# First MLP: the rest of the second half of each weight tile, taken by an accumulating DMA

## The chip, the cores and the metric

The kernel runs on one core of one Trainium2 chip. The metric is the device time of one execution in microseconds (us); a comparison goes by the median of several executions. The trace is one profiled execution, and every time in it counts from the start of its span.

The engines go by the profile's names: PE (TensorE's matmuls), PEld (its weight loads), DVE (VectorE), ACT (ScalarE), POOL (GpSimd), SP (SyncE). Each works through its own list of instructions in order; semaphores tie the lists together.

## The reference

Attention over 4 sequences of 576 rows with 8 heads (a window of 128, a bias that falls with distance), then a first MLP, then a layer of 8 experts that routes each of the 2304 rows to one expert of capacity 288. The change touches the first MLP alone:

```python
def _moe_ref(x, w_in, w_out, alpha):
    h = x @ w_in                                   # 2304 x 512 @ 512 x 2048
    g = np.maximum(h, 0.0) + alpha * np.minimum(h, 0.0)
    return (g @ w_out).astype(np.float32)          # 2304 x 2048 @ 2048 x 512
```

## The kernel before

**Tiles.** The first MLP's hidden dimension is cut into 16 tiles `f` of 128. Tile `f` of the weights is one array of 128 partitions by 1024 numbers: its first half (columns 0 to 511) is the part of `w_in`, its second half (512 to 1023) the part of `w_out`. The rows of `x` are cut into 9 units `u` of 256.

**Splitting.** The weights lie in memory as 64-bit numbers, and the matmuls take pairs of float32r parts: `wh` (a weight, rounded) and `wl` (the rest, weight minus `wh`). `load_w64` fetches 1 MB, one tile, as 16-bit words (`raw`); one transfer of SP's queue for tiles 0 to 2, of ACT's queue for the others. `split_w64_(f, i)` then makes half `i` of tile `f`: DVE takes the top words of both halves at once (L144, or L142 for each half of tile 15), ACT makes the first bits of `w` (L149), DVE adds the mantissa (L150) and the sign (L151), ACT writes `wh` as a rounded copy of `w` (L152), and POOL writes `wl` as `w - wh` (L153). `w` is tile `w64w`, of which there are two buffers, under the tag that the output tiles `y` use later. Tile 15 is loaded in two halves of 0.5 MB through one buffer (`raw15_0`, `raw15_1`); the constants `ramps` (an IOTA of POOL, L722) take that buffer afterwards.

**Work.** `l1(u, f)` is 12 matmuls of 256 columns (`wh` with `xh`, `wh` with `xl`, `wl` with `xh`) on the first half; ACT (L557) and DVE (L558) make the activation `g` from it, ACT the rounded `gh` (L561), and for units 0 and 1 POOL the rest `gl` (L565). `l2(u, f)` multiplies `gh` and `gl` with the second half of the tile, `wh` and `wl`. Units 0 and 1 alternate over the tiles, unit 0 four tiles ahead: `l1(0, f)` is number `2f - 2` of these steps from tile 4 on. So tile 9 comes into use at the 16th `g`, tile 11 at the 20th, tile 15 at the 28th. From the 33rd on, units 2 to 8 use weights that are all there.

**Order.** The attention of later blocks goes on among these steps. The code gives a rough order; a scheduler with its own idea of durations then places each instruction on its engine and assigns the buffers. Of tile `f` from 4 on, the load stands behind the instruction kept in `SPLIT[f - 2]`:

```python
g = LOADED.get(LG_) if f == LF else SPLIT.get(f - LD) if f > LF else None   # LF = 3, LD = 2
with tc.issue_after(g.ins) if g is not None else nullcontext():
    load_w64_(f)
```

## Time and profile before

| | |
|---|---|
| runs | 933.4, 936.16, 939.03 us; median 936.16 us |
| the profiled execution | 942.45 us, of which the span of the trace is 939.7 us |
| PE busy in the span | 846.7 us (90%) |
| DVE, ACT, POOL busy | 626.6 us (67%), 472.7 us (50%), 363.5 us (39%) |
| granted TensorE clock, mean | 0.942 |

The shares are averages over an attention stage with the first MLP (to about 580 us) and an expert stage behind it. The change works in the first 165 us, so what counts is which engine is full there, and for what PE waits there.

### The profile page before, as it was taken

What the parts mean: (1) busy time and instruction counts of PE and PEld (TensorE: products, weight loads), DVE (VectorE), ACT (ScalarE), POOL (GpSimd) and SP (SyncE); (2) the same over time, 40 slices, a digit from 0 to 9 for tenths busy, and PEclk for the clock granted to TensorE, in tenths of its full rate; (3) what the DMA queues carried; (4) which work ended last, traced back from release to release, by engine and by line L of the source; (5) the groups of instructions that cost most, each with busy time, mean ns of one, the idle gap of its engine ahead of it and who ended that gap; (6) DMA issues with size and microseconds to landing.
All of it is one profiled execution on the core that took longest, in us unless ns stands there. A gap on an engine that the chain in (4) does not pass through costs nothing.

```text
span 939.7 us, 18007 instructions
## 1 busy us (share of the span) xinstructions
PE 846.7 (90%) x6709; PEld 774.9 (82%) x6709; DVE 626.6 (67%) x1709; ACT 472.7 (50%) x1131; POOL 363.5 (39%) x316
## 2 busy tenths in 40 slices
PE   6797788999999999999999999398979889799996
PEld 4676666888898999899999998387969788699996
DVE  7899996367776877887776544677677666762210
ACT  4787776565655656565655333134325243244541
POOL 5656666421101101110000000196566774659841
PEclk8999999999999999999999999568889889799999
DMA  7753452012211212112010000245343353436510
GB/s 210 250 180 131 144 169 85 20 49 80 73 42 58 74 29 80 58 35 79 13 35 1 19 5 14 80 135 164 129 141 125 107 167 130 120 121 182 180 49 25
DMA packets 33911, 89.00 MB, mean 95 GB/s; under 512 B 7456, under 2 KB 7456, under 8 KB 33824
## 3 DMA queue, kind: packets, MB, share of 16 engines
q1 hardware_dynamic: 28736, 64.79, 22.3%
q10 hardware_dynamic: 2016, 13.63, 4.2%
q0 software_dynamic: 3072, 9.44, 3.2%
q8 instruction: 52, 0.85, 0.4%
q14 instruction: 35, 0.29, 0.1%
HBM read 78.40 MB, written 9.44 MB: 93 GB/s over the span
## 4 chain that ended last, share of the span: by engine, by line
PE 71%; DVE 20%; DMA 3%; SPq 2%; issue 2%; ACT 1%; POOL 0%; POOLq 0%; DVEq 0%; ACTq 0%
PE ph L551 18%; PE py L593 16%; PE pyx L1098 11%; PE phx L1080 10%; DVE cmp L864 5%; PE prt L878 3%; DVE w64w L151 3%; DVE w64w L150 3%; PE S L408 2%; PE py L579 2%; PE pav L502 2%; DVE w64q L144 2%; PE pt L443 1%; PE prt L1002 1%; PE pox L1116 1%
## 5 line engine op out<-in xcount | busy, mean ns | idle before, releaser
L551 PE MATMUL ph<-xh,ws 128*128 128x256 f32 x1152 | 188.0, 286 | 12.1 <-DVE g L558 11.9
L1032 POOL TENSOR_TENSOR ws<-wr,ws 128x512 fp32r<-128x512 f32 x128 | 166.3, 1332 | 55.0 <-ACT ws L1029 54.6
L551 PEld LDWEIGHTS ph<-xh,ws 128*128 128x128 f32 x1152 | 160.0, 190 | 25.8 <-DVE g L558 19.6
L593 PE MATMUL py<-ws,gh 128*128 128x512 f32 x512 | 151.2, 404 | 1.5 <-ACT gh L561 1.5
L343 POOL TENSOR_TENSOR ks<-kr,ks 64x512 fp32r<-64x512 f32 x34 | 51.5, 1518 | 217.5 <-ACT ks L342 197.9
L558 DVE SCALAR_TENSOR_TENSOR g<-ph,sa_sb,g 128x256 f32<-128x256 f32 x144 | 68.9, 480 | 75.3 <-ACT g L557 75.0
L557 ACT ACTIVATE g<-ph,sg_sb 128x256 f32<-128x256 f32 x144 | 67.5, 470 | 97.8 <-PE ph L551 94.3
L1098 PE MATMUL pyx<-hh,ws 128*128 128x288 f32 x512 | 116.5, 313 | 0.0
L1029 ACT ACTIVATE ws<-wr 128x512 fp32r<-128x512 f32 x128 | 72.9, 628 | 56.0 <-DMA wr<-in_we_dram 54.3
L593 PEld LDWEIGHTS py<-ws,gh 128*128 128x128 f32 x512 | 88.7, 190 | 14.6 <-ACT gh L561 2.0
L561 ACT ACTIVATE gh<-g,sg_sb 128x256 fp32r<-128x256 f32 x144 | 72.7, 506 | 50.8 <-DVE g L558 27.8
L551 PE MATMUL ph<-xl,ws 128*128 128x256 f32 x576 | 96.4, 282 | 0.0
L1080 PE MATMUL phx<-exh,ws 128*128 128x288 f32 x512 | 92.2, 321 | 0.0
L593 PE MATMUL py<-ws,gl 128*128 128x512 f32 x256 | 89.5, 409 | 1.4 <-POOL gl L565 1.1
L1098 PEld LDWEIGHTS pyx<-hh,ws 128*128 128x128 f32 x512 | 89.9, 200 | 0.0
L551 PEld LDWEIGHTS ph<-xl,ws 128*128 128x128 f32 x576 | 81.7, 190 | 2.2
L864 DVE TENSOR_TENSOR cmp<-ramps,u 128x1280 f16<-128x1280 f16 (+5 forms) x58 | 81.1, 1438 | 0.2
L1080 PEld LDWEIGHTS phx<-exh,ws 128*128 128x128 f32 x512 | 80.2, 207 | 0.4 <-ACT exh L1051 0.3
L1098 PE MATMUL pyx<-hl,ws 128*128 128x288 f32 x256 | 78.7, 307 | 0.0
L567 DVE SCALAR_TENSOR_TENSOR gl<-g,sg_sb,gh 128x256 fp32r<-128x256 f32 x112 | 58.3, 523 | 18.2 <-ACT gh L561 16.1
L878 PE MATMUL prt<-ob,cmp 128*128 128x8 f16 x522 | 38.1, 205 | 35.3 <-DVE cmp L864 32.9
L878 PEld LDWEIGHTS <-cmp 128*128 128x128 f16 x522 | 35.4, 161 | 39.3 <-DVE cmp L864 35.2
(251 smaller groups left out, 1662.2 us busy)
## 6 DMA issues: line engine op xcount, KB each, us to landing
wr<-in_we_dram SPq DMA_DIRECT2D x64, 512.0 KB, 3.6
raw<-in_wm_dram ACTq DMA_DIRECT2D x12, 1023.8 KB, 5.6
kr<-in_k_dram SPq DMA_DIRECT2D x68, 128.0 KB, 2.8
qr<-in_q_dram SPq DMA_DIRECT2D x64, 128.0 KB, 2.7
y_dram<-y SPq DMA_DIRECT2D x18, 256.0 KB, 2.3
vr<-in_v_dram SPq DMA_DIRECT2D x13, 256.0 KB, 3.0
raw<-in_wm_dram SPq DMA_DIRECT2D x3, 1023.8 KB, 8.1
whole<-in_v_dram SPq DMA_DIRECT2D x4, 256.0 KB, 5.6
```

The source lines that it names most:

```text
L551: nc.tensor.matmul(ph, w[f][:, c * P:(c + 1) * P], x[u][:, c, :], start=i == 0, stop=i == 11)
L557: nc.scalar.activation(g, ph, AF.Copy, scale=sg)
L558: nc.vector.scalar_tensor_tensor(g, ph, sa_sb[:, f:f + 1], g, op0=ALU.mult, op1=ALU.max)
L561: nc.scalar.activation(gh, g, AF.Copy, scale=sg)
L567: nc.vector.scalar_tensor_tensor(gl, g, sg, f32(gh), op0=ALU.mult, op1=ALU.subtract)
L593: nc.tensor.matmul(PY[u][i], a[:, s], w[f][:, 512:], start=f == 0 and j == 0, stop=f == FT - 1 and j == 2)
L864: nc.vector.tensor_tensor(cmp[:, :K, cs], th[:, :, :n], u16[:, None, cs].to_broadcast([P, K, n]), ALU.is_le)
L878: nc.tensor.matmul(cnt, cmp[:, :, c], r["ob"][:, c], start=c == 0, stop=c == NB - 1)
L1029: nc.scalar.activation(wh[s][:, h], w[:, h], AF.Copy)
L1032: (nc.vector if on_dve else nc.gpsimd).tensor_sub(wl[s][:, h], w[:, h], f32(wh[s][:, h]))
L1080: nc.tensor.matmul(ph, w[s][:, c * P:(c + 1) * P], x[:, c], start=i == 0, stop=i == 11)
L1098: nc.tensor.matmul(py, w[s][:, cs], r[x][f], start=i == 0, stop=i == 23)
```

## The change

The first half of each tile is made as before. For the second half ACT writes, behind `wh`, a second copy `-w`, rounded in the same way, to the place of `wl`; POOL then issues a DMA that adds `w` to it in SBUF, so that `w - wh` stands there when it has landed. `SPLIT[f]`, behind which the load of tile `f + 2` stands, is now that second copy.

```diff
@@ -150,7 +150,12 @@
         SPLIT[f] = nc.scalar.activation(wh[f][:, s], w, AF.Copy)
-        nc.gpsimd.tensor_sub(wl[f][:, s], w, f32(wh[f][:, s]))
+        if i == 0:
+            nc.gpsimd.tensor_sub(wl[f][:, s], w, f32(wh[f][:, s]))
+        else:
+
+            SPLIT[f] = nc.scalar.activation(wl[f][:, s], w, AF.Copy, scale=-1.0)
+            nc.gpsimd.dma_start(f32(wl[f][:, s]), w, accum_op=ALU.add)
```

The lines below 153 move down by 5 in the changed kernel: L558 becomes L563, L722 becomes L727, and the new copy and the new DMA are L157 and L158.

The first place is DVE about the 16th `g`. Before, it is `g_1247` below, and the halves of tiles 12 to 14 (`raw12`, `raw13`, `raw14`) stand around it:

```order
L150 SCALAR_TENSOR_TENSOR w64w_1381<-raw12_1227,w64w_1381 128x512
L151 SCALAR_TENSOR_TENSOR w64w_1381<-raw12_1227,w64w_1381 128x512
L144 TENSOR_SCALAR w64q_1416<-raw13_1344 128x1024
L558 SCALAR_TENSOR_TENSOR g_1247<-ph_644,sa_sb_100,g_1247 128x256
L150 SCALAR_TENSOR_TENSOR w64w_1418<-raw13_1344,w64w_1418 128x512
L151 SCALAR_TENSOR_TENSOR w64w_1418<-raw13_1344,w64w_1418 128x512
L150 SCALAR_TENSOR_TENSOR w64w_1496<-raw13_1344,w64w_1496 128x512
L558 SCALAR_TENSOR_TENSOR g_1316<-ph_644,sa_sb_100,g_1316 128x256
L151 SCALAR_TENSOR_TENSOR w64w_1496<-raw13_1344,w64w_1496 128x512
L144 TENSOR_SCALAR w64q_1535<-raw14_1424 128x1024
```

In the changed kernel the 16th `g` is `g_1258` on DVE, and the halves around it are those of tiles 9 and 10:

```order
L150 SCALAR_TENSOR_TENSOR w64w_1111<-raw9_982,w64w_1111 128x512
L144 TENSOR_SCALAR w64q_1151<-raw10_1052 128x1024
L151 SCALAR_TENSOR_TENSOR w64w_1111<-raw9_982,w64w_1111 128x512
L150 SCALAR_TENSOR_TENSOR w64w_1153<-raw10_1052,w64w_1153 128x512
L151 SCALAR_TENSOR_TENSOR w64w_1153<-raw10_1052,w64w_1153 128x512
L563 SCALAR_TENSOR_TENSOR g_1258<-ph_648,sa_sb_100,g_1258 128x256
L563 SCALAR_TENSOR_TENSOR g_1328<-ph_648,sa_sb_100,g_1328 128x256
L150 SCALAR_TENSOR_TENSOR w64w_1196<-raw10_1052,w64w_1196 128x512
L144 TENSOR_SCALAR w64q_1230<-raw11_1159 128x1024
L151 SCALAR_TENSOR_TENSOR w64w_1196<-raw10_1052,w64w_1196 128x512
```

The splitting has moved back against the rest. Counted over DVE's whole list, 26 halves (L150) stand ahead of the 16th `g` before and 21 now, 31 and 24 ahead of the 20th, 32 and 28 ahead of the 24th, 32 and 32 ahead of the 28th. What else stands ahead of each of these is the same on PE, DVE and ACT, but for a few rows.

The second place is ACT between two loads. Before, with the semaphores that a row waits for (`Pool` is POOL's, `DVE` DVE's, `DMAHW` a load's), the second half of tile 10 begins (L149 of `w64w_1186`) ahead of the `wh` of its first half:

```order
L149 ACTIVATE w64w_1186<-w64q_1141,least_75 128x512 [waits Pool_49]
L152 ACTIVATE ws10_1140<-w64w_1143 128x512 [waits DMAHW6_49,DVE_49]
L561 ACTIVATE gh_1029<-g_1026,sg_sb_99 128x256 [waits DVE_49]
L564 ACTIVATE g_1026<-g_1026,sg_sb_99 128x256 [waits Activation_49]
L557 ACTIVATE g_1063<-ph_644,sg_sb_99 128x256 [waits PE_49]
L149 ACTIVATE w64w_1221<-w64q_1219,least_75 128x512 [waits DVE_49,Pool_49]
L152 ACTIVATE ws10_1140<-w64w_1186 128x512 [waits DVE_49]
L122 DMA raw12_1227<-in_wm_dram 128x4095 [waits DMAHW2_49]
```

In the changed kernel, on ACT again (`DMASW` is an accumulating DMA's semaphore):

```order
L152 ACTIVATE ws10_1150<-w64w_1153 128x512 [waits DMAHW7_49,DVE_49]
L566 ACTIVATE gh_1261<-g_1258,sg_sb_99 128x256 [waits DVE_49,Pool_49]
L569 ACTIVATE g_1258<-g_1258,sg_sb_99 128x256 [waits Activation_49]
L562 ACTIVATE g_1328<-ph_648,sg_sb_99 128x256 [waits PE_49]
L149 ACTIVATE w64w_1196<-w64q_1151,least_75 128x512 [waits Pool_49]
L566 ACTIVATE gh_1331<-g_1328,sg_sb_99 128x256 [waits DVE_49]
L569 ACTIVATE g_1328<-g_1328,sg_sb_99 128x256 [waits Activation_49]
L149 ACTIVATE w64w_1232<-w64q_1230,least_75 128x512 [waits DMASW1_49,DVE_49]
L562 ACTIVATE g_1376<-ph_648,sg_sb_99 128x256 [waits PE_49]
L152 ACTIVATE ws10_1150<-w64w_1196 128x512 [waits DVE_49]
L157 ACTIVATE ws10_1150<-w64w_1196 128x512
L122 DMA raw12_1238<-in_wm_dram 128x4095 [waits DMAHW3_49]
```

Both halves of a tile now take the same `w64w` buffer, one behind the other: the second half's L149 (`w64w_1196`) stands behind the first half's L152 and waits for POOL's L154 on it; tile 11's first L149 (`w64w_1232`) waits for the accumulating DMA of tile 9; and the load of tile 12 stands behind both copies of tile 10's second half.

The third place is the end of the splitting on POOL. In the changed kernel (before, L153 of `ws15` stands where L158 does now):

```order
L154 TENSOR_TENSOR ws15_1631<-w64w_1634,ws15_1631 128x512
L570 TENSOR_TENSOR gl_1776<-g_1772,gh_1775 128x256
L570 TENSOR_TENSOR gl_1822<-g_1818,gh_1821 128x256
L727 IOTA ramps_3007 128x1280
L727 IOTA ramps_3007 128x768
L570 TENSOR_TENSOR gl_1848<-g_1844,gh_1847 128x256
L158 DMA ws15_1631<-w64w_1713 128x512
```

The last accumulating DMA stands behind the two IOTA and a `gl`, and PE's first product with that part stands behind the 31st `l1` of its list.

## Rows read from the trace of the kernel before

**Rows 1.** The page, section 1: busy us of each engine, share, instructions.

```profile
PE 846.7 (90%) x6709; PEld 774.9 (82%) x6709; DVE 626.6 (67%) x1709; ACT 472.7 (50%) x1131; POOL 363.5 (39%) x316
```

**Rows 2.** By stretch: length; busy PE, PEld, DVE, ACT, POOL; clock, DMA, GB/s.

```profile
60.00:140.00 80.00, 65.86 (x402) 54.21 (x402) 78.69 (x146) 57.14 (x135) 51.96 (x43) 0.96 0.45 149
140.00:165.00 25.00, 21.07 (x123) 16.15 (x123) 17.00 (x25) 16.88 (x34) 15.73 (x13) 1.00 0.27 85
165.00:182.00 17.00, 16.54 (x100) 13.56 (x99) 3.32 (x7) 8.66 (x18) 9.27 (x9) 1.00 0.00 1
```

**Rows 3.** PE's waits from 60 to 140 us: total, times, longest.

```profile
PE ph L551 <- DVE g L558: 5.9, 7, 1.4
PE pav L494 <- DVE et L472: 2.6, 4, 1.5
PE S L408 <- DVE mn L431: 2.1, 3, 1.0
```

**Rows 4.** Groups on DVE from 60 to 140 us: busy, mean ns, idle before.

```profile
L151 DVE SCALAR_TENSOR_TENSOR w64w<-raw,w64w 128x512 uint16<-128x512 uint16 x18 | 20.4, 1134 | 0.1
L150 DVE SCALAR_TENSOR_TENSOR w64w<-raw,w64w 128x512 int32<-128x512 int32 x18 | 17.0, 943 | 0.3 <-ACT w64w L149 0.2
L144 DVE TENSOR_SCALAR w64q<-raw 128x1024 uint16<-128x1024 uint16 x9 | 12.0, 1330 | 0.0
```

**Rows 5.** The splitting's instructions: shortest, median, longest in ns.

```profile
L149 ACT ACTIVATE w64w<-w64q,least x32: 704/712/727, 13.1 to 160.2; 128x512 int32<-128x512 uint16 x32
L150 DVE SCALAR_TENSOR_TENSOR w64w<-raw,w64w x32: 649/830/1753, 13.9 to 161.0; 128x512 int32<-128x512 int32 x32
L151 DVE SCALAR_TENSOR_TENSOR w64w<-raw,w64w x32: 690/1148/1856, 17.3 to 162.3; 128x512 uint16<-128x512 uint16 x32
L152 ACT ACTIVATE ws<-w64w x32: 615/630/640, 19.4 to 163.0; 128x512 fp32r<-128x512 f32 x32
...
L144 DVE TENSOR_SCALAR w64q<-raw x15: 667/694/2224, 12.3 to 145.5; 128x1024 uint16<-128x1024 uint16 x15
```

**Rows 6.** Groups on POOL up to 180 us.

```profile
L153 POOL TENSOR_TENSOR ws<-w64w,ws 128x512 fp32r<-128x512 f32 x32 | 44.5, 1393 | 26.9 <-ACT ws L152 21.5 <-issue 4.9 <-POOL ks L343 0.2
L565 POOL TENSOR_TENSOR gl<-g,gh 128x256 fp32r<-128x256 f32 x26 | 25.9, 1000 | 17.4 <-ACT g L564 11.6 <-issue 3.1 <-POOL ws L153 2.1
...
L722 POOL IOTA ramps<- 128x1280 f16 (+1 forms) x2 | 5.6, 2831 | 0.8 <-DVE w64w L151 0.8
```

**Rows 7.** Timeline, ACT and its queue: the load of tile 13.

```profile
133.06 0.63 ACT L152 ACTIVATE ws<-w64w 128x512 fp32r<-128x512 f32 x1 [0.82 <-DVE w64w L151]
133.07 0.34 ACTq L122 DMA_DIRECT2D raw<-in_wm_dram  x1
```

**Rows 8.** The source line of the loads: shortest, median, longest landing.

```profile
DMA to landing us min/median/max: 4.9/5.9/8.1
```

**Rows 9.** Timeline, DVE: tile 13's first step; the 16th, 28th, 31st g.

```profile
139.02 1.23 DVE L144 TENSOR_SCALAR w64q<-raw 128x1024 uint16<-128x1024 uint16 x1
140.17 0.47 DVE L558 SCALAR_TENSOR_TENSOR g<-ph,sa_sb,g 128x256 f32<-128x256 f32 x1
...
181.10 0.48 DVE L558 SCALAR_TENSOR_TENSOR g<-ph,sa_sb,g 128x256 f32<-128x256 f32 x1 [2.35 <-ACT g L557]
...
191.33 0.48 DVE L558 SCALAR_TENSOR_TENSOR g<-ph,sa_sb,g 128x256 f32<-128x256 f32 x1 [1.98 <-ACT g L557]
```

**Rows 10.** Timeline, expert stage: an issue of POOL, and PE's wait for it.

```profile
611.73 0.92 POOL L1014 DMA_INDIRECT xg<-y_dram,ix  x1 [0.30 <-issue]
...
614.86 0.42 PE L1065 MATMUL ptx<-ident,xg 96*128 96x96 f32 x1 [0.39 <-DMA xg<-y_dram,ix]
```

**Rows 11.** Timeline, ACT's queue and DVE: the second half of tile 15.

```profile
156.02 0.33 ACTq L122 DMA_DIRECT2D raw<-in_wm_dram  x1
...
159.70 0.43 DVE L142 TENSOR_SCALAR w64q<-raw 128x512 uint16<-128x512 uint16 x1 [0.52 <-DMA raw<-in_wm_dram]
...
162.25 0.73 DVE L151 SCALAR_TENSOR_TENSOR w64w<-raw,w64w 128x512 uint16<-128x512 uint16 x1
```

## The prediction

> **What bounds the kernel now.** The page's first section makes PE the full engine over the span [rows 1], so a change matters by the idle time of PE that it takes away or adds. The busy time by stretch says where that is: from 60 to 140 us PE is busy 65.9 of 80 us and DVE 78.7, so DVE is full and PE stands still for 14.1; from 140 to 165 us 3.9 us are left; from 165 us on PE is at 16.5 of 17 and DVE at 3.3, so PE is the bound from there [rows 2]. PE's waits in the first of these stretches name the cause: 5.9 us for DVE's `g`, 2.6 and 2.1 us for other products of DVE, 10.6 together [rows 3]. What fills DVE there is the splitting of the weights: 20.4 + 17.0 + 12.0 = 49.4 of its 78.7 us, for 18 halves [rows 4]. The splitting ends long before it is needed: the second half of tile 15 is done on DVE at 163 us [rows 11], and the 28th `g`, the first that needs tile 15, comes at 181.1 us [rows 9]. So DVE spends the time in which PE starves on weights that are not due yet.
>
> **The sum is made by two clocks:** when the 16th `g` comes (140.2 us before) and when the 28th does (181.1 us) [rows 9]; behind it PE is full in both kernels and the work is the same, so what the 28th gains or loses, the end does.
>
> **Up to the 16th `g`.** A half costs DVE 0.94 + 1.13 + 1.33/2 = 2.74 us [rows 4]. Five fewer stand ahead of it now: 13.7 us. Besides, DVE's instructions of the splitting run at 943, 1134 and 1330 ns here where their shortest take 649, 690 and 667 [rows 4, 5]: 18 x 0.29 + 18 x 0.44 + 9 x 0.66 = 19.2 us above them, while POOL is busy for 52 us [rows 2]. I take POOL's work for the cause, since L151 takes from 690 to 1856 ns at one size [rows 5]. Removing half of the 18 L153 takes 9 x 1.39 = 12.5 us from POOL [rows 6], 24% of its 52, and so 4.6 us from DVE. DVE could give back 18.3 us, more than the 14.1 that PE has idle; but PE waits for DVE in 10.6 us of it alone, and for `g` in 5.9. I take the middle of these two, 8.3 us: the 16th `g` at 131.9 us. Bounds: 5.9 and 14.1. ACT's second copy, 16 x 0.63 us [rows 5], lies in its idle time here (57.1 of 80 us busy [rows 2]); without that cover it were 5 us in this stretch.
>
> **From the 16th to the 28th.** The lead is used up here: 11 halves are left where 6 were, and the changed order makes a loop of each tile. In ACT's list the load of tile `f + 2` stands behind L149 of tile `f + 1`, then L152 and L157 of tile `f`. L149 needs L144 of tile `f + 1`, which needs its load. So from one L144 to the next: L144 0.69, L149 0.71, L152 0.63 [rows 5], then the load, which is issued as the copy ahead of it starts (133.07 beside 133.06 us [rows 7]), and 5.9 us to its landing, the median [rows 8]: 7.9 us. Before, the load of tile 13 stood behind one copy and its L144 followed 5.95 us later [rows 7, 9]. The accumulating DMA sets out right behind the load; it reads 0.25 MB twice and writes it once beside the load's 1 MB. Landings go from 4.9 to 8.1 us [rows 8], so the period is 6.9 to 10.1; I take 8.2, with 0.3 us for the new traffic, since these landings already include other transfers (DMA share 0.45 [rows 2]). The Trainium skill ("DMA: Bandwidth & Descriptors", section "Issuing engines are not separate DMA queues") says that DMAs of all issuing engines run on the same 16 DMA engines and interleave. By that rule the load would be stretched by the other's share of the bytes, up to 0.75 to 1, and a period at its upper bound would cost 4 x 1.9 = 7.6 us more (an estimate); no run here shows it yet. DVE has room in this period: two halves at their shortest and two `g` of 0.47 [rows 9] are 4.3 us.
>
> Tile 11's L144 stands behind the 17th `g`, some 3 us behind the 16th. Four periods later, less 2.2 us because tile 15 comes in halves that take 3.7 instead of 5.9 us [rows 11, 8], is tile 15's first step: 131.9 + 3 + 4 x 8.2 - 2.2 = 165.5. Then 0.43 for it [rows 11], 0.71 + 0.65 + 0.69 + 0.63 [rows 5], 1.39 for POOL's subtraction [rows 6], and 2.35 for the matmuls and ACT's pass, which DVE waits for at the 28th `g` [rows 9]: 6.9 us. The 28th `g` comes at 172.4 instead of 181.1: **8.7 us gained**. The clock was 0.96 and 1.00 in these stretches [rows 2]; I leave it so.
>
> **The end of the splitting.** The last accumulating DMA has two IOTA of 2.83 and a `gl` of 1.0 us ahead of it on POOL [rows 6]. From tile 15's first step: 2.5 us for its first half, 3.7 for the load of the second, 3.3 to the end of its L151 (159.70 to 162.98 [rows 11]), 5.7 + 1.0 on POOL, and the DMA. For that the nearest row is POOL's indirect DMA: from its issue at 611.73, which took 0.92, to PE's start at 614.86 us are 3.1 us [rows 10]. Together 19.3 us. PE wants the part behind the 31st step: 6.9 us to the 28th `g` and 10.2 from there (181.10 to 191.33 [rows 9]), 17.1 us. PE waits 2.2 us; 2.5 with the handing over. What is queued behind it on PE is everything else, so it counts in full.
>
> **The sum:** -8.7 + 2.5 = -6.2 us. Against the profiled execution 942.45 - 6.2 = 936.3; that execution lies above the median of the runs, 936.16, so what I forecast is 936.16 - 6.2 = **930.0 us**.
>
> **The unknown price: the accumulating DMA.** Its time `L`, from issue to landing, is 3.1 us by the row above; from the other side, behind a load that lands late, 0.9 + 8.1 = 9.0. It also holds the buffer: tile `f + 2` begins when that of tile `f` has landed, and until its own lands come L149, L150, L151, L152, the subtraction, L149, L150, L144, L151, L152, L157 and a `gl`, 9.1 us from the same rows, 9.5 with the handing over. So two periods are at least 9.5 + `L` + what each step waits in its engine's line. With 3.1 it is 6.3 us a tile and hidden behind the load's 8.2; it takes over from `L` + waiting = 6.9.
>
> **Rivals.**
> *Slower: the buffer's loop becomes the bound.* Six links wait for another engine, and POOL's subtraction, on which the second half now waits, stands behind `gl`. For it speaks that ACT's L149, when it waits, holds up `gh`, `g` and L152 behind it; against it that DVE is no longer full. With `L` = 9 and 5 us of waiting a tile takes 11.75 us, 3.55 more than in the sum: 14.2 us over four tiles. In the 72 us from 60 us to the 16th `g`, 13 halves (18 less five), 6.5 tiles, would need 76: 4.5 us more. -6.2 + 18.7 = +12.5: 948.7 us. It decides (0.5% slower) from `L` + waiting = 12.3.
> *No change: the same loop at half that.* `L` + waiting = 9.9, a tile in 9.7 us: 4 x 1.5 = 6 us, 936 us. One form of it: POOL's issue is held up beside DVE. L144 has POOL's work beside it when it takes 1.33 instead of 0.67 us [rows 4, 5]; if the issue stands as long, subtraction and `gl` behind it come 1.3 us later each tile, 5 us over four: 935. The Trainium skill ("SBUF — State Buffer", section "SBUF: two separate sides") says that a DVE instruction in a two-port mode keeps GpSimd from writing a DMA's descriptors; no run here shows whether L144 does.
> *More: all idle time of PE comes back.* The 16th `g` at 126.1 us and 7.5 us a tile: the 28th at 163.8, 17.3 us gained, less 2.5: 921.4 us. Against it: a quarter of PE's waits are not for DVE.
>
> **Chances.** The forecast (925 to 935) 0.40, no change 0.25, slower 0.25, more 0.10. About 0.5%, 4.7 us, is what a measurement of this kernel can tell from no change. Of the forecast's 0.40 I put 0.30 below 931.5 and 0.10 above; so faster 0.40, same 0.35, slower 0.25. The range leaves out a tenth at each end: 921 to 947. It takes in the bounds of the 16th `g` and a period of 7.5 to 11.5 us; the forecast's own is 925 to 935.
>
> **What would show it.** Right: the 16th `g` near 132 us, L144 of tiles 11 to 15 some 8 us apart, each about 6 us behind its load; L150 and L151 shorter in the mean; the 28th `g` at 172; one wait of PE of 2 to 3 us for the last accumulating DMA. Wrong: L149 idle for `DMASW` or for L154 in each tile, landings of the accumulating DMA above 7 us, PE's products waiting for them in several tiles; or the 16th `g` where it was, in which case DVE wasn't what PE lacked.

## The result and the profile after

The changed kernel took 942.32 us in the median of 11 runs (939.71 to 949.06), the kernel before 936.31 us in 11 runs on the same chip: a ratio of 1.0068, with a 95% interval of 1.0044 to 1.0093. It is **slower by 6 us**, where 6 us faster was forecast. The profiled execution took 943.4 us, its span 941.7.

The page's first section, to be held against [rows 1]: PE, DVE and POOL are busy for less time, PEld for 2.5 us more, and ACT for 6.1 more with its 16 new copies.

```profile
PE 843.7 (90%) x6709; PEld 777.4 (83%) x6709; DVE 621.1 (66%) x1709; ACT 478.8 (51%) x1147; POOL 349.4 (37%) x316
```

The stretches of [rows 2] in the changed kernel, and one more behind them:

```profile
60.00:140.00 80.00, 68.69 (x450) 59.02 (x448) 68.45 (x146) 62.82 (x147) 44.59 (x45) 0.98 0.59 170
140.00:165.00 25.00, 19.82 (x108) 16.21 (x108) 12.82 (x21) 16.76 (x32) 9.78 (x13) 0.93 0.50 138
165.00:182.00 17.00, 11.92 (x59) 9.72 (x59) 7.36 (x14) 9.57 (x20) 6.14 (x7) 0.90 0.34 72
182.00:260.00 78.00, 74.12 (x622) 65.56 (x621) 56.30 (x161) 47.29 (x121) 19.78 (x15) 1.00 0.22 65
```

The last of these in the kernel before:

```profile
182.00:260.00 78.00, 76.96 (x652) 68.98 (x650) 57.03 (x162) 48.42 (x122) 15.58 (x12) 1.00 0.23 72
```

Two halves show. Up to 140 us the change does what was forecast: DVE falls from 78.7 to 68.5 us and PE rises from 65.9 to 68.7. Behind it PE stands still more than before, 10.3 us instead of 4.4 from 140 to 182 us and 3.9 instead of 1.0 from there to 260, with a DVE that has plenty of idle time. So from 140 to 182 us no engine is full: a chain of waits bounds the kernel there.

PE's waits from 140 to 182 us name the chain (before there was only one kind, for `g`):

```profile
PE ph L556 <- DVE g L563: 5.5, 6, 2.0
PE py L598 <- DMA ws<-w64w: 5.0, 4, 2.6
```

The source line of the accumulating DMA, over the whole span: the issue on POOL, who waited for the landing (us, times), and the time from issue to landing:

```profile
L158 POOL DMA_DIRECT2D ws<-w64w x16: 862/867/1120, 22.8 to 188.4; - x16
...
  PE py L598: 8.3, 7
  ACT w64w L149: 5.6, 5
DMA to landing us min/median/max: 3.7/5.5/7.4
```

A landing takes 3.7 to 7.4 us, inside the bounds of 3.1 to 9.0 that the prediction gave `L`. Both waits that the prediction wrote down as signs against itself are here: ACT's first step of a half waits for it, and PE in several tiles.

**Where the time goes, by stage.** The starts of certain `g` on DVE cut the first stage into pieces that repeat well from one execution to the next. The kernel before was profiled once more (e9 below), the changed kernel twice more: once as it is (e17), once with an edit that alters no order (e1). The later traces come from other chips, on which the kernel before took 941.5 to 942.4 us in the median, not 936.3. All in us:

| | 4th `g` at | 4th to 16th | 16th to 28th | 28th to 144th | from there to the end |
|---|---|---|---|---|---|
| before, two traces | 70.6, 74.5 | 69.6, 70.0 | 40.9, 40.9 | 398.6, 398.3 | 360.0, 360.4 |
| changed, three traces | 65.3, 68.6, 63.3 | 65.1, 64.0, 65.4 | 50.5, 49.5, 49.3 | 403.1, 405.2, 405.1 | 357.6, 362.5, 361.0 |

By the means, 6.8 us are gained to the 4th `g` and 4.9 from there to the 16th; 8.9 are lost from the 16th to the 28th and 6.0 behind it. Together 3.2 us lost, of the 6 that the medians tell; the rest lies within the scatter of the first column, some 4 us for one and the same kernel, and the interval of the medians, 2.3 us to either side.

### The profile page after: what moved, and what is told of

Its sections match the earlier page's. It is cut to its first block, busy times and chain, and to the rows that moved or that the text cites. A ratio compares the mean times of both kernels' runs of the same rounds, so it can differ in the third digit from the quotient of the medians.

```text
span 941.7 us, 18071 instructions
## 1 busy us (share of the span) xinstructions
PE 843.7 (90%) x6709; PEld 777.4 (83%) x6709; DVE 621.1 (66%) x1709; ACT 478.8 (51%) x1147; POOL 349.4 (37%) x316
## 4 chain that ended last, share of the span: by engine, by line
PE 68%; DVE 16%; DMA 7%; ACT 3%; SPq 2%; issue 2%; POOL 1%; POOLq 0%; ACTq 0%; DVEq 0%
PE ph L556 17%; PE py L598 16%; PE pyx L1103 11%; PE phx L1085 8%; DVE cmp L869 6%; DMA ws<-w64w 4%; PE prt L883 3%; PE S L413 2%; PE py L584 2%; DMA vr<-in_v_dram 2%; PE pav L507 2%; DVE w64w L150 1%; PE pt L448 1%; DVE ql L334 1%; DVE g L995 1%
## 5 line engine op out<-in xcount | busy, mean ns | idle before, releaser
L1037 POOL TENSOR_TENSOR ws<-wr,ws 128x512 fp32r<-128x512 f32 x128 | 169.0, 1353 | 46.9 <-ACT ws L1034 46.4
L598 PE MATMUL py<-ws,gh 128*128 128x512 f32 x512 | 156.6, 410 | 9.2 <-DMA ws<-w64w 8.3
L563 DVE SCALAR_TENSOR_TENSOR g<-ph,sa_sb,g 128x256 f32<-128x256 f32 x144 | 69.1, 480 | 73.3 <-ACT g L562 73.0
L598 PEld LDWEIGHTS py<-ws,gh 128*128 128x128 f32 x512 | 89.3, 191 | 25.4 <-DMA ws<-w64w 10.9
L598 PE MATMUL py<-ws,gl 128*128 128x512 f32 x256 | 90.2, 408 | 1.3 <-POOL gl L570 1.0
L1085 PE MATMUL phx<-exh,ws 128*128 128x288 f32 x512 | 88.1, 310 | 0.0
L1085 PEld LDWEIGHTS phx<-exh,ws 128*128 128x128 f32 x512 | 76.3, 198 | 0.4 <-ACT exh L1056 0.3
```

The source lines that it names most:

```text
L563: nc.vector.scalar_tensor_tensor(g, ph, sa_sb[:, f:f + 1], g, op0=ALU.mult, op1=ALU.max)
L598: nc.tensor.matmul(PY[u][i], a[:, s], w[f][:, 512:], start=f == 0 and j == 0, stop=f == FT - 1 and j == 2)
L1037: (nc.vector if on_dve else nc.gpsimd).tensor_sub(wl[s][:, h], w[:, h], f32(wh[s][:, h]))
L1085: nc.tensor.matmul(ph, w[s][:, c * P:(c + 1) * P], x[:, c], start=i == 0, stop=i == 11)
```

## The experiments

The ratios are to runs of the kernel before on the same chip, with 95% intervals; the runs used several chips. Two theories stood from the start. **B** (buffers): the accumulating DMA costs time because it holds a `w64w` buffer, of which there are two, and the next half can't begin. **L** (landing): it costs time because something waits for the landing as such, or for its traffic, wherever the splitting stands. G, A, P, Z and T are named where they were tried.

The table gives what was measured. "Halves" are those ahead of the 16th, 20th and 24th `g` on DVE, and `g` the start of the 28th and of the 144th in the trace.

| run | halves | 28th `g` | 28th to 144th | 144th `g` | ratio |
|---|---|---|---|---|---|
| before (two traces) | 26, 31, 32 | 181.1, 185.4 | 398.6, 398.3 | 579.7, 583.8 | 1 |
| changed | 21, 24, 28 | 180.9 | 403.1 | 584.0 | 1.0068 (1.0044 to 1.0093) |
| e1 gate | 21, 24, 28 | 182.2 | 405.2 | 587.3 | 1.0068 (1.0043 to 1.0093) |
| e2 third buffer | 26, 30, 32 | 178.1 | 398.8 | 576.9 | 1.0014 (0.9993 to 1.0036) |
| e3 no DMA | 31, 32, 32 | 183.6 | 398.6 | 582.2 | 1.0060 (1.0038 to 1.0083) |
| e4 both halves | 21, 25, 29 | 190.5 | 398.1 | 588.6 | 1.0115 (1.0076 to 1.0154) |
| e5 DMA to tile 7 | 22, 27, 31 | 179.4 | 399.6 | 579.0 | 1.0031 (1.0005 to 1.0057) |
| e6 DMA to tile 9 | 21, 25, 30 | 176.9 | 400.4 | 577.3 | 1.0012 (0.9983 to 1.0041) |
| e7 DMA from tile 10 | 26, 29, 32 | 179.7 | 399.4 | 579.1 | 0.9999 (0.9971 to 1.0026) |
| e8 one buffer | 20, 24, 28 | 206.6 | 399.9 | 606.6 | 1.0311 (1.0282 to 1.0339) |
| e10 third buffer late | 22, 27, 31 | 177.7 | 399.6 | 577.3 | 1.0024 (0.9996 to 1.0051) |
| e11 the same, GpSimd late | 22, 27, 31 | 180.3 | 399.9 | 580.2 | 1.0017 (0.9992 to 1.0042) |
| e12 loads earlier | 21, 24, 29 | 177.7 | 402.9 | 580.5 | 1.0071 (1.0046 to 1.0096) |
| e13 DMA to tile 11 | 21, 24, 28 | 179.0 | 399.6 | 578.7 | 0.9953 (0.9922 to 0.9985) |
| e14 tile 15 by GpSimd | 21, 24, 28 | 180.7 | 400.0 | 580.7 | 1.0024 (0.9998 to 1.0050) |
| e15 DMA to 9, loads earlier | 21, 25, 29 | 179.1 | 400.2 | 579.3 | 0.9984 (0.9956 to 1.0011) |
| e16 DMA to 11, gate | 21, 24, 28 | 176.5 | 399.6 | 576.1 | 1.0000 (0.9982 to 1.0018) |
| e17 changed, again | 21, 24, 28 | 178.1 | 405.1 | 583.3 | 1.0061 (1.0030 to 1.0091) |

**e1: the loads' wait undone.**

```diff
-            SPLIT[f] = nc.scalar.activation(wl[f][:, s], w, AF.Copy, scale=-1.0)
+            nc.scalar.activation(wl[f][:, s], w, AF.Copy, scale=-1.0)
```

> The changed kernel, but the load of tile f + 2 stands behind the copy wh again, not behind the second copy -w. Every engine keeps its order; only this wait changes. Theory G (the later load stretches the tiles): each load sets out 0.6 to 1 us earlier, tile 15's first step comes 3 to 5 us earlier, the 28th g near 177 us instead of 181, and the time falls to 937 to 939 us. Theory B (the two w64w buffers, each held by both halves of a tile until the accumulating DMA has landed) and theory L (PE waits for the landing itself) both expect 941 to 943 us, no change against the changed kernel, with ACT's first half still waiting for the accumulating DMA.

1.0068, the changed kernel's ratio again, and the 28th `g` at 182.2 us, not near 177: theory G falls. That the load stands behind one copy more costs nothing that shows.

**e2: a third buffer.**

```diff
-        w = mlp.tile([P, 512], F32, name="w64w", tag="y", bufs=2)
+        w = mlp.tile([P, 512], F32, name="w64w", tag="y" if i else "y2", bufs=2 if i else 1)
```

> The changed kernel with a third buffer for w: second halves take the two that there were, first halves take one of their own, under the tag of a tile that is first used after the 33rd g. The accumulating DMAs stay, all 16 of them. The splitting stands as far ahead as before the change again: 26 halves ahead of the 16th g (21 in the changed kernel), 30 ahead of the 20th. Theory B (the buffers are what the DMA's time costs): the splitting is done before 170 us, PE's waits for the accumulating DMA nearly vanish, the 28th g comes at 174 to 178 us, and the time is 930 to 936 us, 6 to 12 below the changed kernel. Theory L (the DMA's landing of 5.5 us and its traffic cost the time wherever the splitting stands): PE still waits for it in several tiles, 940 to 943 us.

The 28th `g` came at 178.1 us and nothing was lost behind it; 1.0014, so nearly all of the loss is gone with all 16 DMAs in place. In the whole trace no engine waits for one of them; these two lines are all that PE waits for between 140 and 260 us:

```profile
PE ph L556 <- DVE g L563: 4.2, 6, 1.3
PE py L598 <- POOL gl L570: 1.6, 2, 1.3
```

B expected the loss to go. But the third buffer brings the lead back too, so this run alone can't say which of the two did it. B also hoped for a gain, and that did not come: with 26 halves ahead of the 16th `g` again, the early gain is mostly gone.

**e3: no DMA.**

```diff
-            nc.gpsimd.dma_start(f32(wl[f][:, s]), w, accum_op=ALU.add)
```

> The changed kernel without the accumulating DMA; the second half's wl is left at -w, so the output is not the reference's. The second copy on ACT and half of the subtractions on POOL stay as in the changed kernel. Theories B and L: the loss is the DMA's, so this is faster than the kernel before, 925 to 933 us, and PE waits neither for the DMA nor much for DVE. Theory A (ACT's 16 additional copies, or their place in its line, are the loss): 939 to 943 us, as the changed kernel.

1.0060: B and L missed. The ratio is the one that A expected, but A falls with e2, which has all 16 copies and loses 0.1%. Without the DMA the scheduler puts 31 halves ahead of the 16th `g`, five more than before, and in the trace that `g` starts at 147.1 us, 2.6 and 6.9 us behind the two traces of before, 14 to 18 behind the changed kernel. The stretch from 60 to 140 us shows it, with DVE full and PE less busy than before although POOL has 14 us less to do:

```profile
60.00:140.00 80.00, 62.41 (x376) 53.45 (x375) 77.12 (x153) 60.69 (x142) 37.97 (x33) 0.91 0.51 167
```

So taking work off POOL doesn't help where it lets the splitting run still further ahead. With 21, 26 and 31 halves ahead, the 16th `g` comes at 129 to 133, 137 to 145 (e2 and both of before) and 147 us: some 1.5 us for each half. By the piece from the 4th to the 16th alone (61 to 66, 68 to 70 and 73 us) it is half of that; the rest stands ahead of the 4th. At the 28th and the 144th `g` this trace lies between the two of before (183.6 and 582.2 us), so where the 0.6% of the median is lost, it doesn't show.

**e4: twice the dose.**

```diff
-        if i == 0:
+        if i < 0:
             nc.gpsimd.tensor_sub(wl[f][:, s], w, f32(wh[f][:, s]))
```

> The accumulating DMA for both halves of each tile: twice as many of them, twice the copies -w, no subtraction on POOL. Theory L (each landing costs PE its wait): twice the loss or more, 948 us and above. Theory B (buffers): each half holds its buffer for some 3.3 us of work and 5.5 us of landing, 9 to 10 us with the waits, and there are two buffers and two halves to a tile, so a tile takes 9 to 10 us instead of the changed kernel's mean of 8.6; the 28th g near 187 us, 945 to 952 us. Both expect slower; what tells them apart is where PE waits: for the first half's DMA ahead of l1 (L) or for g (B).

1.0115, and the 28th `g` at 190.5: slower, by about what both expected. From 140 to 260 us PE waits 9.8 us for `g` and 4.9 for the DMA, all of these in the product with the second half (L598) and none ahead of `l1`: B's sign, not L's.

**e5, e6 and e7: some of the tiles.** `f >= 8` (e5), `f >= 10` (e6) or `f < 10` (e7) is added to the condition, so that GpSimd subtracts there:

```diff
-        if i == 0:
+        if i == 0 or f >= 8:
             nc.gpsimd.tensor_sub(wl[f][:, s], w, f32(wh[f][:, s]))
```

> The accumulating DMA for tiles 0 to 7 alone; from tile 8 on GpSimd subtracts both halves, as before the change. 22 halves stand ahead of the 16th g (21 in the changed kernel, 26 before), but 31 ahead of the 24th (28 and 32). Theory P (the smaller lead and the lighter POOL gain some 12 us by the 20th g, and the late tiles' loop through the DMA and its buffers gives them back): with the loop gone the gain stays. The 20th g 8 to 12 us earlier than before the change, the 28th 5 to 9 us, time 5 to 8 us under the kernel before (ratio 0.992 to 0.995). Theory Z (what is postponed has to be paid before the 28th g whatever makes the rest): the 28th g within 2 us of before, ratio 0.998 to 1.003.

> As the run before, with the DMA for tiles 0 to 9: 21 halves ahead of the 16th g, 25 ahead of the 20th, 30 ahead of the 24th. Theory P: the same gain at the 20th g (10 to 12 us), two more tiles in the slow loop, the 28th g 3 to 7 us earlier than before, ratio 0.994 to 0.998. Theory Z: ratio 0.998 to 1.003.

> The other part alone: the accumulating DMA for tiles 10 to 15 only. 26 halves ahead of the 16th g as before the change, 29 ahead of the 20th. Theory P: nothing is gained up to the 16th g (within 2 us), and the late loop costs: the 28th g 3 to 8 us later than before, ratio 1.004 to 1.010. Theory T (the loss is the tail, the last tiles' DMA behind the IOTA and what stands behind the 28th g): the 28th g within 2 us, then 3 to 5 us lost behind it, ratio 1.003 to 1.006. If the lead alone decides (it is there again up to the 20th): ratio 1.000.

The DMA in the tiles to 9 costs nothing that can be told (e6, 1.0012), and in the late ones nothing either (e7, 0.9999: the case in which the lead alone decides, and PE never waits for a DMA); all 16 together cost 0.7%. So the loss is of neither part but of their meeting: the early tiles spend the lead, and the late ones then can't afford the DMA. e5 doesn't quite fit: with fewer DMAs than e6 it loses 0.3%, by an interval that just leaves out 1, and its trace, with the 144th `g` at 579.0 us, does not show where. P's hope for a gain fell, though: in e6 the 20th `g` came 9.4 us earlier than in the first trace of before, and 4.2 were left at the 28th, 2.4 at the 144th. In e5 it was 7.3 at the 20th and 2.5 at the 24th. Here Z is nearer.

**e8: one buffer, no DMA.** The kernel before with the buffers cut:

```diff
-        w = mlp.tile([P, 512], F32, name="w64w", tag="y", bufs=2)
+        w = mlp.tile([P, 512], F32, name="w64w", tag="y2", bufs=1)
```

> The kernel before with one buffer for w instead of two, so GpSimd makes all of wl, with no DMA and no second copy. The scheduler's order comes to nearly the lead of the changed kernel: 20 halves ahead of the 16th g, 24, 28 and 31 ahead of the 20th, 24th and 28th. Theory P in the form 'the lost lead with its loop of buffers loses, not the DMA's landing': the 16th g 3 to 7 us earlier than before (no relief of POOL), a tile in 8.5 to 9 us, the 28th g 0 to 4 us later than before, ratio 1.000 to 1.006. In the form 'the DMA's landing loses': the 28th g 3 to 6 us earlier than before, ratio 0.993 to 0.998, with PE never waiting for wl.

1.0311. It was meant to give the changed kernel's lead without its DMA, and it overshot: a tile takes 10 us (its first steps at 146.7, 156.7, 166.6, 176.6), so nothing follows for the DMA. It prices a loop of buffers that is too tight, without any DMA: 29.7 us.

**e9: the kernel before, a second look.**

> The kernel before once more, for a second profiled execution of it: the first one lies 6 us above the median of its runs. If its excess stands in the first stage, the 144th g comes 3 to 6 us earlier than 579.7 here; if it stands in the expert stage (from the first expert product to the end 323.9 us in the first), the 144th g comes within 1.5 us of 579.7 and the expert stage is shorter.

The 144th `g` at 583.8, 4.1 us later than in the first trace, the expert stage 360.4 us against 360.0. Neither case came: the difference stands ahead of the 4th `g` alone (74.5 against 70.6), as the table of stages shows. So the pieces between the 4th and the 144th `g` can be compared between kernels, and the time of the 4th only roughly.

**e10 and e11: the third buffer from tile 10 on,** with all the DMAs (e10), and with GpSimd from tile 10 on (e11):

```diff
-        w = mlp.tile([P, 512], F32, name="w64w", tag="y", bufs=2)
+        w = mlp.tile([P, 512], F32, name="w64w", tag="y" if i or f < 10 else "y2", bufs=2 if i or f < 10 else 1)
```

> The changed kernel, all 16 accumulating DMAs, with the third buffer for w from tile 10 on alone. Up to the 16th g the order is that of the changed kernel (22 halves ahead of it, 21 there), then the splitting gains lead again: 27 ahead of the 20th, 31 ahead of the 24th (24 and 28 in the changed kernel). Theory B (a DMA's time costs only through the buffer that it holds while the splitting has no lead): the gain up to the 20th g stays, 8 to 12 us, the 28th g comes 2 to 6 us earlier than in the kernel before's trace, PE's waits for the accumulating DMA and the 3 us lost behind the 28th g vanish; ratio 0.998 to 1.003. Theory L (the landing itself, which PE waits for): as in the changed kernel, ratio 1.005 to 1.009.

> The run before with GpSimd subtracting both halves from tile 10 on, as before the change; the same buffers, and the same lead at the 16th, 20th and 24th g (22, 27, 31). What is between the two is six accumulating DMAs against six subtractions. Theory B: within 0.3% of each other. Theory L: this one faster by 0.3 to 0.6%. Both: the 20th g 8 to 12 us earlier than in the kernel before's trace; if that gain lasts to the end the ratio is 0.992 to 0.997, if it is paid back by the 28th g as in the two runs that mix DMA and GpSimd, 0.999 to 1.003.

1.0024 and 1.0017, on one chip: no difference that can be told between six DMAs and six subtractions where there is a buffer for them, so L falls. PE doesn't wait for the DMA in e10 from 140 us on (ahead of that it waits 4.5 us once behind the 16th `g`, and e11, which has the DMA to tile 9 too, 4.3):

```profile
PE ph L556 <- DVE g L563: 5.0, 8, 1.9
PE py L598 <- POOL gl L570: 1.1, 2, 0.7
```

The early gain isn't kept here either: the 20th `g` came at 148.9 and 153.2 us (before 155.9 and 160.2, changed 143.7), since the halves that were put off are now made between the 16th and the 24th.

**e12: loads earlier.** `LD` is 3 instead of 2, so the load of tile `f` stands behind the copies of `f - 3`.

> The changed kernel with the load of tile f behind the second copy of tile f - 3 instead of f - 2. Nearly the same order (21, 24, 29 halves ahead of the 16th, 20th, 24th g). The prediction's loop (each tile's first step waits for a load that stands behind the copy of two tiles earlier, 8.2 us a tile) says that the late tiles come closer, 7 to 7.5 us, the 28th g 4 us earlier than in the changed kernel, ratio 1.002 to 1.005. Theory B (the loop is that of the two buffers and the accumulating DMA): no change, ratio 1.005 to 1.009, and 7.5 to 8.5 us a tile.

1.0071. The first steps of tiles 10 to 15 stand 7.6, 7.9, 9.9, 7.8 and 7.4 us apart, much as in the changed kernel (7.5, 8.0, 9.9, 7.3 and 7.9 in e17), though each comes 13.5 to 18.5 us behind its load, not 5.5 to 9: the loads don't pace them, and the prediction's loop through the load is not the one that ran.

**e13 and e14: the last four tiles, and the last one, by GpSimd** (`f >= 12`, `f == FT - 1` in the condition as in e5).

> The changed kernel with GpSimd subtracting both halves of tiles 12 to 15; two buffers, and exactly the changed kernel's lead (21, 24, 28 halves ahead of the 16th, 20th, 24th g). So against the changed kernel only the last four accumulating DMAs and copies -w are gone, no lead and no buffer is added. If the DMA's time in the buffers' loop is what loses (5.5 us of landing against 1.4 of a subtraction), the late tiles come 1 to 2 us closer, the 28th g 4 to 6 us earlier than in the changed kernel, nothing is lost behind it, ratio 1.000 to 1.003. If the lost lead loses by itself, whoever makes wl, ratio 1.005 to 1.009.

> The changed kernel with GpSimd subtracting both halves of tile 15 alone; the same lead. If the tail (the last DMA behind the two IOTA, and the 3 us behind the 28th g) makes half of the loss, ratio 1.002 to 1.004, with the 28th g as in the changed kernel and nothing lost behind it. If the loss is made by tiles 10 to 14 and the tail only hands it on: ratio 1.005 to 1.008.

In e14 DVE's order is that of the changed kernel up to the 34th `g`, in e13 up to the 23rd, and no lead is added. Without the DMA of tile 15 little is lost behind the 28th `g` (400.0 us, against 403.1 to 405.2) and the ratio is 1.0024, the first of its two cases: by the medians two thirds of the loss are gone, though the interval touches that of the changed kernel. Without the last four it was 0.9953, under the range of its first case, with the 28th `g` only 1.9 us earlier than in the changed kernel's first trace and nothing lost behind it. So over the whole the lost lead does not lose by itself: from the 16th to the 28th `g` it costs what it gained ahead of that (48.3 us in e13, 40.9 before).

**e15: a try at more.** e6 with `LD` 3.

> A try at a better kernel: accumulating DMA for tiles 0 to 9, each load behind the copy of tile f - 3. In the run with the DMA to tile 9, DVE waited 3.3 us for the last load between 140 and 182 us, and the 28th g came 4.2 us ahead of the kernel before's trace. If the late tiles are then paced by their loads, 2 to 4 us more are gained and the ratio is 0.994 to 0.999; if they are paced by the halves' own chain through ACT, DVE and POOL, it stays at 0.999 to 1.003.

0.9984 (0.9956 to 1.0011), inside the range of the first case, and its interval holds both. What the first case rests on didn't come: the tiles from 11 on stood 6.9 to 7.1 us apart, but the 28th `g` came no earlier (179.1 us, 176.9 in e6).

**e16 and e17: on one chip.** e16 is e13 with the edit of e1; e17 is the changed kernel.

> The kernel with the accumulating DMA for tiles 0 to 11, with the loads behind the copy wh as before the change; every engine's order is that of the run without this edit, and in the changed kernel the same edit made no difference (1.0068 with and without). If the last four DMAs in the buffers' loop are what loses, and the rest of the change gains a little, ratio 0.993 to 0.998 as there. If that run's 0.9953 was scatter (the run with the DMA to tile 9 gave 1.0012, with the first stage as long), ratio 0.999 to 1.003.

> The changed kernel once more, on the chip of the run beside it: what the last four accumulating DMAs cost, on one chip. If they are the loss: 1.004 to 1.009, and 0.7 to 1.2% above the run beside it, with the 144th g 5 to 9 us later than there. If the two are within 0.4% of each other, the cause isn't settled.

1.0000 (0.9982 to 1.0018) against 1.0061 (1.0030 to 1.0091). The last four accumulating DMAs cost 0.6%, a little less than the 0.7% that was asked for, with intervals that lie apart, and the 144th `g` comes 7.2 us later with them. (The two differ by the edit of e1 as well, which changed nothing there.) PE in the two stretches behind 140 us, first with the DMA to tile 11:

```profile
140.00:182.00 42.00, 34.93 (x190) 27.82 (x189) 26.74 (x44) 26.84 (x56) 23.90 (x19) 0.92 0.28 82
182.00:260.00 78.00, 76.84 (x646) 68.65 (x644) 56.65 (x165) 48.63 (x124) 16.88 (x14) 1.00 0.24 72
```

and the changed kernel on the same chip:

```profile
140.00:182.00 42.00, 30.74 (x175) 25.07 (x173) 19.86 (x34) 26.51 (x53) 18.07 (x18) 0.96 0.39 102
182.00:260.00 78.00, 74.22 (x611) 65.86 (x610) 56.90 (x159) 45.93 (x117) 17.41 (x15) 0.98 0.22 65
```

That the rest of the change gains 0.5%, as e13 had it, is not confirmed: e16 is the case in which 0.9953 was scatter.

## Why the prediction was wrong, point by point

**What bounds the kernel up to the 16th `g`: right, its number in part by luck.** DVE was full, and what it was full of mattered. With five halves fewer ahead of it the 16th `g` came at 130.4 us in the changed kernel's first trace, 131.9 were forecast; the other two have 132.7 and 128.8. But three of the five fewer halves stand ahead of the 4th `g` already (8 there, 11 before), and 6.8 of the 11.7 us that the means gain come ahead of it, where one kernel's traces are 4 us apart:

```profile
130.39 0.48 DVE L563 SCALAR_TENSOR_TENSOR g<-ph,sa_sb,g 128x256 f32<-128x256 f32 x1 [0.33 <-ACT g L562]
```

**POOL beside DVE: the right cause, too small, and by the wrong measure.** The groups of [rows 4] in the changed kernel: L151 went from 1134 to 873 ns in the mean, L150 from 943 to 785, L144 from 1330 to 695. Over 16 halves and 8 tiles that is 4.2 + 2.5 + 5.1 = 11.8 us, more than the 4.6 that were put down for it. POOL's work was 7.4 us less in this stretch (44.6 against 52.0). The prediction took DVE's loss in proportion to that work, and the proportion doesn't hold: in e3 POOL is busy for 38.0 us only, and L144 still takes 1257 ns in the mean.

```profile
L151 DVE SCALAR_TENSOR_TENSOR w64w<-raw,w64w 128x512 uint16<-128x512 uint16 x16 | 14.0, 873 | 0.1
L150 DVE SCALAR_TENSOR_TENSOR w64w<-raw,w64w 128x512 int32<-128x512 int32 x16 | 12.6, 785 | 1.4 <-ACT w64w L149 1.2
...
L144 DVE TENSOR_SCALAR w64q<-raw 128x1024 uint16<-128x1024 uint16 x8 | 5.6, 695 | 0.0
```

What decides is which of the two starts first. Before, one L144 beside one of POOL's subtractions, which had started 0.49 us earlier:

```profile
138.53 1.16 POOL L565 TENSOR_TENSOR gl<-g,gh 128x256 fp32r<-128x256 f32 x1 [0.74 <-POOL ws L153]
139.02 1.23 DVE L144 TENSOR_SCALAR w64q<-raw 128x1024 uint16<-128x1024 uint16 x1
```

and in the changed kernel, where POOL starts second:

```profile
126.79 0.69 DVE L144 TENSOR_SCALAR w64q<-raw 128x1024 uint16<-128x1024 uint16 x1
127.34 0.74 POOL L570 TENSOR_TENSOR gl<-g,gh 128x256 fp32r<-128x256 f32 x1 [1.46 <-ACT g L569]
```

From 60 to 140 us, 6 of the 9 L144 before start while a subtraction of POOL is running, and each ends 0.54 to 0.56 us after that subtraction does (1.23 to 2.22 us long); the other three take 0.67 to 0.69. In the changed kernel one of 8 starts so, with 0.08 us of the subtraction left, and none takes more than 0.78. L151 lies beside an issue of the accumulating DMA 6 times there and takes 0.74 to 0.77 us, as it does alone (0.72 to 0.77).

**From the 16th to the 28th: the step that failed.** Forecast were 40.5 us (131.9 to 172.4), measured 49.3 to 50.5, and so nearly all of the forecast gain went. In the prediction's own terms, over the three traces of the changed kernel: tile 11's first step came 3.9 to 4.0 us behind the 16th `g` (3 forecast), tile 15's 33.1 to 34.6 us behind that (30.6 forecast), and the 28th `g` 11.9 to 12.5 us behind that (6.9 forecast). So the last link is the term that was furthest off, and the period of the tiles comes next. The experiments show what made them longer.

*Half or more of it comes with the lost lead, not with the DMA.* In e5 and e6 GpSimd makes the late tiles, no matmul of PE waits for a DMA in this piece, and it takes 47.8 and 46.1 us; in e13 and e16, with the changed kernel's lead and the DMA to tile 11, 48.3 and 48.0. In the runs that keep the lead (before, e2, e3, e7) it takes 36.5 to 40.9, with and without the DMA. PE's waits for `g` in the piece, first before, then in e6:

```profile
PE ph L551 <- DVE g L558: 4.3, 9, 1.5
```

```profile
PE ph L556 <- DVE g L563: 9.7, 10, 1.8
```

The prediction let every us gained at the 16th `g` stand, and only asked when tile 15 would be ready: its late tiles are 8.2 us apart, and PE is not held up by the halves on their way. But the halves that were put off lie among the `g` again: DVE is busy for 32.5 us of the piece in e6, 19.2 before. From 140 to 182 us PE is busy for 34.9 us at a mean clock of 0.92 in e16, 37.6 at 1.00 before [rows 2]: multiplied, an estimate, some 5.5 us of PE's work less in the same time.

*The rest is the loop of the two buffers.* Against e13 and e16 it is 1 to 2.5 us by the lengths of the piece. But the granted clock over the piece was 0.93 in these two, in e5 and in the changed kernel's first trace, 0.98 in e1 and e17, and 1.00 in e6 and before, so PE's idle time compares better: 4.4 us before, 8.7 and 9.7 in e5 and e6, 7.8 to 8.1 in e13 and e16, 11.2 to 13.1 in the three traces of the changed kernel, of which PE's matmuls wait 5.0 to 6.2 for the DMA. By that the late DMAs add 1.5 to 5 us of idle time to the 3 to 5 of the lost lead. The prediction had seen this loop and set it aside: "With 3.1 it is 6.3 us a tile and hidden behind the load's 8.2; it takes over from `L` + waiting = 6.9." `L` was taken at the nearest row, an indirect DMA of 3.1 us, and waiting at nothing. One turn can be read from the timeline: tile 12's first step on ACT waits for the DMA of tile 10, tile 12's own DMA is issued by POOL, and tile 14's first step, which by ACT's list waits for it, comes right as it has landed:

```profile
144.68 0.72 ACT L149 ACTIVATE w64w<-w64q,least 128x512 int32<-128x512 uint16 x1 [2.11 <-DMA ws<-w64w]
...
156.62 0.87 POOL L158 DMA_DIRECT2D ws<-w64w  x1 [3.31 <-ACT ws L157]
...
161.81 0.73 ACT L149 ACTIVATE w64w<-w64q,least 128x512 int32<-128x512 uint16 x1
```

Two tiles in 17.1 us, 8.6 each; by the prediction's own formula, (9.5 + `L` + waiting)/2, `L` + waiting is 7.6, of which the landing is about 5.0. So this loop took over from the load's, and e12 agrees, since earlier loads changed nothing. The loads themselves, which the prediction let grow by the new traffic, landed in 3.7 to 8.5 us with a median of 5.3, no slower than before [rows 8]. Two signs of being right came true by this other loop: the first steps some 8 us apart, and each 5.5 to 9 us behind its load.

And the last link was the wrong one. The prediction followed tile 15's own first half from its first step to the 28th `g`, 6.9 us; it was 11.9 to 12.5. Ahead of it in PE's line stands the product with tile 14's second half, for which the prediction had no term. The chain in the changed kernel, every link with what it waited for:

```profile
167.67 0.72 ACT L149 ACTIVATE w64w<-w64q,least 128x512 int32<-128x512 uint16 x1 [1.14 <-DMA ws<-w64w]
...
168.43 0.69 DVE L150 SCALAR_TENSOR_TENSOR w64w<-raw,w64w 128x512 int32<-128x512 int32 x1 [2.45 <-ACT w64w L149]
...
169.92 0.74 DVE L151 SCALAR_TENSOR_TENSOR w64w<-raw,w64w 128x512 uint16<-128x512 uint16 x1
...
170.72 0.61 ACT L152 ACTIVATE ws<-w64w 128x512 fp32r<-128x512 f32 x1
...
171.24 0.62 ACT L157 ACTIVATE ws<-w64w 128x512 fp32r<-128x512 f32 x1
...
172.15 0.87 POOL L158 DMA_DIRECT2D ws<-w64w  x1 [2.44 <-ACT ws L157]
...
178.16 0.74 PE L598 MATMUL py<-ws,gh 128*128 128x512 f32 x2 [1.70 <-DMA ws<-w64w]
178.20 0.73 ACT L149 ACTIVATE w64w<-w64q,least 128x512 int32<-128x512 uint16 x1 [0.31 <-DMA ws<-w64w]
...
180.91 0.48 DVE L563 SCALAR_TENSOR_TENSOR g<-ph,sa_sb,g 128x256 f32<-128x256 f32 x1 [1.16 <-ACT g L562]
```

The second half of tile 14 begins when tile 13's DMA has landed (167.67 us). Its own DMA is issued at 172.15 and lands at 178.1; PE then goes on, the 28th `g` follows 2.75 us later, and ACT begins the second half of tile 15 in the same moment. One landing holds up two engines, each with its line behind it.

**The end of the splitting: a term of 2.5 us that was 4.5 to 6.9, in another form.** Forecast was one wait of 2.5 us of PE for the last DMA. That DMA was issued at 188.4 us, and PE's matmuls did not stand for it. But the piece behind the 28th `g` is 4.5 to 6.9 us longer than in the two traces of before, and this is the greater part of the net loss. So the premise that what the 28th `g` gains the end gains too failed as well. PE stands still for 3.8 to 3.9 us of this piece, 0.8 to 1.0 before, and its busy time is longer too, 399.2 us in the first trace and 401.3 and 401.4 in e1 and e17, with a clock of 0.99, against 397.6. What PE waits for there are other things, of which the longest is this one, in which DVE stands 2.67 us for a load of the attention (L357) with the instruction behind it that PE wants:

```profile
226.18 0.69 DVE L357 TENSOR_REDUCE vc<-vr 128x1 f32<-128x512 f32 x1 [2.67 <-DMA vr<-in_v_dram]
226.78 0.68 DVE L691 TENSOR_TENSOR yt<-pty,y 128x512 f32<-128x512 f32 x1
...
227.52 0.66 PE L448 MATMUL pt<-ident,e 128*128 128x128 f32 x4 [1.85 <-DVE yt L691]
```

The four traces with this loss (changed, e1, e12, e17) all have this wait of PE, of 1.6 to 1.9 us, and the same shorter ones beside it; of the other 15 only e15 has it, with 0.2 us. In the four, DVE's next instruction behind `yt` is `yl` (L693); in e14 and e4 it is a `g`, and PE doesn't wait. With tile 15's DMA alone gone (e14), DVE's order is another one from the 34th `g` on, and 3 to 5 us are back. With a third buffer (e2, e10) they are back too, with all the DMAs. And e4, with the latest last DMA of all (192.5 us), two buffers and no lead, loses nothing there (398.1 us). So the loss goes with the order that the scheduler gave to what follows, not with the landing of the last DMA. That the order makes it is argued: no run changed that order alone.

**Clock.** It was left as it was. From 140 to 182 us the granted clock had been 1.00; it was 0.93 and 0.90 in the two stretches of the changed kernel's first trace, 0.96 over both in e17. That PE waited more doesn't settle it: e6, with 9.7 us of idle time from the 16th to the 28th `g`, kept 1.00 there.

**The rivals.** The slower rival named a loop that did take over, that of the buffers, but with the wrong reach: it was to decide from `L` + waiting = 12.3, and it was slower at 7.6, which by the prediction's formula costs some 1.4 us over four tiles. The lost lead, the last link and the piece behind the 28th `g` made the rest. The form of the second rival in which POOL's issue stands beside DVE falls: the 16 issues took 0.86 to 1.12 us, so none was held up by 1.3 us. The rival in which all of PE's idle time comes back was furthest off.

**What stays open.** In e16 the 144th `g` comes 3.6 and 7.7 us ahead of the two traces of before, and yet the medians are equal. The expert stage took 363.2 us there against 360.0 and 360.4, but it lies between 357.6 and 366.3 over all traces, with the same instructions, so one trace can't tell whether it gives something back. And e13 and e16, which differ by an edit that made no difference elsewhere, are 0.5% apart with intervals that hardly meet, on two chips; e6 has the same first stage and 1.0012.

## What to carry to other kernels

A transfer that takes the place of an engine's instruction holds its source buffer until it has landed. Count the turn of that buffer with the landing and the waits in it, before calling the transfer hidden, and ask of the last users of the weights, not of the first alone, which instruction PE has ahead of them. Work that runs far ahead of its use can starve what is due now, but here putting it off only moved the wait, and its lead is also what hides a slower step: here the early tiles could spend it or the late ones could take the slow step, and not both.

## What was not expected of the hardware

One kernel's executions differ ahead of the 4th `g` and then run alike up to the 144th. From 30 to 60 us the granted clock was 0.98 in the first trace of before and 0.68 in the second, which is from another chip, with the same order on every engine:

```profile
30.00:60.00 30.00, 23.69 (x180) 20.89 (x180) 27.73 (x67) 24.37 (x64) 18.78 (x14) 0.98 0.70 225
```

```profile
30.00:60.00 30.00, 25.75 (x143) 24.23 (x143) 26.49 (x56) 20.53 (x53) 16.18 (x13) 0.68 0.57 184
```

From the 4th to the 16th `g` these two took 69.6 and 70.0 us, from the 16th to the 28th 40.9 and 40.9. The changed kernel's three traces lie within 1.4 us of each other in each of the first two of these pieces, within 2.0 from the 28th to the 144th, and within 4.8 in the expert stage. So a difference between kernels that stands ahead of the 4th `g`, or behind the 144th, needs more than one trace of each; one of several us between them shows in one.

VectorE's instruction for the top words (L144, 0.68 us by itself) ends some 0.55 us after GpSimd's subtraction when it starts while that one is running, and loses nothing when it starts first. So what GpSimd cost VectorE here went by which of them started first, not by GpSimd's busy time.
